# An attention decode kernel whose load order becomes K(n+1), V(n), with the values weighted one step later

## The chip, the cores and the metric

The kernel runs on one core of one Trainium2 chip. The metric is device time in microseconds (us) of one execution; lower is better. Before the change the median of three runs is 1319.77 us (1319.67 to 1320.77).

## What is computed

One decode step of a transformer block, batch 4, one query token, 32 heads of 128, a cache of 4096 positions, everything in float32:

```python
mod = (_silu(c) @ w_mod).reshape(c.shape[0], 6, 1, -1)
h = _layernorm(x, axis=-1) * (1 + ca) + sa
q = (h @ wq).reshape(B, Sq, H, Dh).transpose(0, 2, 1, 3)
scores = jnp.einsum("bhqd,bhkd->bhqk", q, k_cache) * (Dh ** -0.5)
p = _softmax(scores, axis=-1)
o = jnp.einsum("bhqk,bhkd->bhqd", p, v_cache)
x = x + ga * (o.transpose(0, 2, 1, 3).reshape(B, Sq, H * Dh) @ wo)
h = _layernorm(x, axis=-1) * (1 + cb) + sb
x = x + gb * (_silu(h @ w1) @ w2)
```

The two caches are 4 x 32 x 4096 x 128 floats, 268 MB each. Everything else is small beside them.

## The kernel before, in words

**Tiles.** The caches are cut into N = 32 steps. Step n takes one batch entry (b = n mod 4) and one group of four heads (t = n div 4); its K tile and its V tile are [128 partitions, 128 positions x 128] floats each, that is 128 x 16384 x 4 bytes = 8.39 MB. I call them K0 to K31 and V0 to V31 (k0, v0 and so on in the listings; the profile leaves the number out).

**Slots.** One such tile fills 64 KB of each partition, and the pool `kv` has three slots. Every big load is a `Slot`: the modulation weights `wm` (first, with the small work tiles of the opening behind them), `wq`, then the K and V tiles, then `wo`, then the FFN weights `w12`. A new slot takes the place of the one that came free first, so a load waits until the last reader of the load three places earlier in the order is done. All loads are issued by SyncE (SP), in the order of the program, in `fetch` (line 85); a load that waits holds up those behind it.

**A step.** In the K part, POOL multiplies the first 40 positions by the query and DVE the other 88 (`mult`, line 280), and DVE sums all of them over the head dimension (`red`, line 285, once for 88 and once for 40). The query that DVE reads is in PSUM (`qb`), that of POOL is a copy in SBUF (`qw`, line 275). Then comes the softmax: a row maximum on DVE (`rowmax`, line 289), a transpose on PE (`bmax`, line 293), three small DVE operations (`negmax`, lines 298 to 301) and the exponential on ACT (`softexp`, line 307); POOL then spreads the weights into the two tiles `pz` (line 311), from which PE takes its stationary operands. In the V part, POOL weights and folds the first 32 positions (`vmult`, lines 323 and 327), PE multiplies the other 96 by `pz` (`pv`, line 348) and adds the folded part with one more matmul (`vsum`, line 333). The last two steps leave all 128 positions to PE. `gather`, `norm` and `spread` turn the sums of a head group into the rows that the output projection reads (`project_a`, `project`).

**Order.** The order on each engine is that in which the program is written (`manual_schedule`). In step n the loop issues the load of K(n+1) first, does the K part and the softmax of n, issues the load of V(n+1), and does the V part of n. `vsum(n - 1)` stands behind the multiplications of step n. So the transfers are K0 V0 K1 V1 ... K31 V31, `wo`, `w12`. K31 is loaded and multiplied in two halves. `w12` comes in nine pieces of falling size, because the last matmuls of the FFN wait for the last of them.

Of the kernel before, what the change touches and what calls it, by code (L numbers as in the profile page):

```python
# [9 lines left out]
F32 = mybir.dt.float32  # L10
# [7 lines left out]
def kernel(  # L18
# [10 lines left out]
    nc = tc.nc  # L29
    P = 128  # L30
    B, H, S, Dh = kc.shape
# [7 lines left out]
    NT = H // HP  # L39
    TA = NT // 2  # L40
    QA = P // (HP * TA)
    RA = Dh // QA
    NJ = HP * S // P
# [6 lines left out]
    NI = F // P  # L50
    FG = F // G
    NA = 40
    NL = 56
    NV = 32
    SCALE = 1.0 / math.sqrt(Dh)
    EPS = 1e-5
    N = B * NT
# [4 lines left out]
    work = ctx.enter_context(tc.tile_pool(name="work", bufs=2))  # L62
# [24 lines left out]
    kt, vt = {}, {}  # L87

    def load(dst, cache, name, n, *cuts):
        t, b = divmod(n, B)  # L90
        dst[n] = Slot(f"{name}{n}").take(NJ, Dh)
        src = cache[b, HP * t : HP * (t + 1)].rearrange("h (p j) d -> (h p) j d", p=QW)
        fetch(dst[n], src, *(cuts or (0, NJ)))

    def load_k(n, *cuts):
        load(kt, kc, "k", n, *cuts)

    def load_v(n):
        load(vt, vc, "v", n)

    s0 = Slot("wm")
    cT, xT = s0.take(NK, B), s0.take(NK, B)
# [160 lines left out]
    qb, qw = {}, {}  # L263

    def make_qb(n):
        if n % B == 0:
            m = work.tile([P, B, Dh], F32, tag="o", name=f"qm{n}", bufs=1)
            for b in range(B):
                nc.scalar.activation(m[:, b, :], qn, AF.Copy, scale=sel[:, n + b : n + b + 1])  # L269
            p = psum([P, B, Dh], "q", 2)  # L270
            nc.tensor.matmul(p, blk.rearrange("p i x -> p (i x)"), m, start=True, stop=True)  # L271
            for b in range(B):
                qb[n + b] = p[:, b, :]
        qw[n] = work.tile([P, Dh], F32, tag="qw", name=f"qw{n}")
        nc.scalar.activation(qw[n], qb[n], AF.Copy)  # L275

    sc, nm, po, rs = {}, {}, {}, {}

    def mult(eng, src, n, lo, hi):
        eng.tensor_mul(  # L280
            kt[n][:, lo:hi, :], kt[n][:, lo:hi, :], src[n].unsqueeze(1).to_broadcast([P, hi - lo, Dh])
        )

    def red(n, lo, hi):
        nc.vector.tensor_reduce(sc[n][:, lo:hi], kt[n][:, lo:hi, :], axis=AX.X, op=ALU.add)  # L285

    def rowmax(n):
        nm[n] = work.tile([P, 1], F32, tag="rm", name=f"rm{n}")
        nc.vector.tensor_reduce(nm[n], sc[n], axis=AX.X, op=ALU.max)  # L289

    def bmax(n):
        p = psum([P, P], "mx", 2)
        nc.tensor.transpose(p, nm[n].to_broadcast([P, P]), ident)  # L293
        nm[n] = p

    def negmax(n):
        m = work.tile([P, HP], F32, tag="hx", name=f"hx{n}")
        nc.vector.tensor_reduce(m, nm[n].rearrange("p (i x) -> p i x", i=HP), axis=AX.X, op=ALU.max)  # L298
        nc.vector.tensor_mul(m, m, hn)
        nm[n] = work.tile([P, 1], F32, tag="nm", name=f"nm{n}")  # L300
        nc.vector.tensor_reduce(nm[n], m, axis=AX.X, op=ALU.add)  # L301

    def softexp(n):
        t, b = divmod(n, B)
        if b == 0:
            rs[t] = work.tile([P, B], F32, tag="rs", name=f"rs{t}")
        nc.scalar.activation(sc[n], sc[n], AF.Exp, bias=nm[n], accum_out=rs[t][:, b : b + 1])  # L307
        for h in range(2):
            f = first(n) if h == 0 else 0
            m = HG - f  # L310
            nc.gpsimd.tensor_mul(  # L311
                pz[h][:, f * W : HG * W].rearrange("p (g x) -> p g x", g=m)[:, :, E:].rearrange("p g (i j) -> p g i j", i=HP),
                sc[n][:, JJ * (HG * h + f) : HG * JJ * (h + 1)].rearrange("p (g j) -> p g j", j=JJ)
                .unsqueeze(2).to_broadcast([P, m, HP, JJ]),
                hm.unsqueeze(1).unsqueeze(3).to_broadcast([P, m, HP, JJ]),
            )

    def first(n):
        return NV // JJ if n < N - 2 else 0

    def vmult(n):
        if first(n):
            nc.gpsimd.tensor_mul(  # L323
                vt[n][:, :NV, :], vt[n][:, :NV, :], sc[n][:, :NV].unsqueeze(2).to_broadcast([P, NV, Dh])
            )
            for m in (NV // 2, NV // 4, JJ):
                nc.gpsimd.tensor_add(vt[n][:, :m, :], vt[n][:, :m, :], vt[n][:, m : 2 * m, :])  # L327

    def vsum(n):
        t, b = divmod(n, B)  # L330
        q, a = divmod(b, 2)
        o = (1 - a) * E
        nc.tensor.matmul(  # L333
            po[t, q][0:W, :], hs[:, o : o + W], vt[n][:, :JJ, :].rearrange("p j d -> p (j d)"),
            start=False, stop=a == 1,
        )

    def pv(n):
        t, b = divmod(n, B)
        q, a = divmod(b, 2)  # L340
        if a == 0:
            po[t, q] = psum([P, JJ * Dh], "po", 2)
        f = first(n)
        for j in range(f, NG):
            g = j % G
            h, u = divmod(j, HG)
            o = u * W + (1 - a) * E
            nc.tensor.matmul(  # L348
                po[t, q][W * g : W * (g + 1), :],
                pz[h][:, o : o + W],  # L350
                vt[n][:, JJ * j : JJ * (j + 1), :].rearrange("p j d -> p (j d)"),
                start=(a == 0 and j < f + G), stop=(a == 1 and j >= NG - G and (g > 0 or not f)),
            )
# [45 lines left out]
    def spread(t):  # L399
        if t < TA:  # L400
            g = slice(W * t, W * (t + 1))
            v = work.tile([P, B, QA, RA], F32, tag="o", name="v", bufs=1)
            nc.vector.tensor_mul(
                v[g], od[t][g].rearrange("p b (q r) -> p b q r", q=QA),
                rd[t][g].unsqueeze(3).to_broadcast([W, B, QA, RA]),
            )
            nc.vector.tensor_reduce(oa[g], v[g].rearrange("p b q r -> p r b q"), axis=AX.X, op=ALU.add)
            return
        on = work.tile([P, R, QW], F32, tag="lnu", name="on", bufs=1)
        nc.vector.tensor_scalar(  # L410
            on, od[t].rearrange("p (x r) -> p r x", r=R), rd[t][:, 1:2], None, op0=ALU.mult
        )
        ot = work.tile([P, R, W], F32, tag="o", name="ot", bufs=1)
        nc.vector.transpose(ot, on)
        nc.vector.tensor_copy(oz[:, t - TA], ot[:, :, :B])
# [9 lines left out]
    def project(lo, hi):  # L425
        for t in range(lo - TA, hi - TA):
            for r in range(R):
                nc.tensor.matmul(
                    accp[W * r : W * r + B, :], oz[:, t, r, :], wot[:, t, r, :],
                    start=False, stop=t == NT - TA - 1,  # L430
                )

    make_qb(0)
    load_v(0)
    for n in range(N):
        t, b = divmod(n, B)
        if n < N - 2:
            load_k(n + 1)
        elif n == N - 2:
            load_k(n + 1, 0, NJ // 2, NJ)  # L440
        else:
            so = Slot("wo")
            wat, wot = so.take(RA, D), so.take(NT - TA, R, D)
            fetch(so.t, wo, 0, RA * D, SLOT - R * D, SLOT)
        sc[n] = work.tile([P, NJ], F32, tag="sc", name=f"sc{n}")
        if n + 1 < N:
            mult(nc.gpsimd, qw, n, 0, NA)
            mult(nc.vector, qb, n, NA, NJ)
            make_qb(n + 1)
            if n and first(n - 1):  # L450
                vsum(n - 1)
            red(n, NA, NJ)
        else:
            for lo in (0, NJ // 2):
                mid, hi = lo + NL // 2, lo + NJ // 2
                mult(nc.gpsimd, qw, n, lo, mid)
                mult(nc.vector, qb, n, mid, hi)
                red(n, mid, hi)
        if n + 1 < N:
            red(n, 0, NA)  # L460
        else:
            for lo in (0, NJ // 2):
                red(n, lo, lo + NL // 2)
        rowmax(n)
        bmax(n)
        negmax(n)
        if t and b == 1:
            spread(t - 1)
        softexp(n)
        if n + 1 < N:  # L470
            load_v(n + 1)
        else:
            s2 = Slot("w12")
            w1t = s2.take(NK, F)
            w2t = s2.take(NI, D)
            fetch(s2.t, w12, 0, 3 * F, *(NK * F + i * D for i in (0, 5, 8, 10, 11, 12, 13, 14)))
        if b == B - 1:
            norm(t)
        vmult(n)
        pv(n)  # L480
        if n and b == 0:
            gather(t - 1, 1)
        if b == 2:
            gather(t, 0)
    project_a()
    gather(NT - 1, 1)
    project(TA, NT - 1)
    spread(NT - 1)
    project(NT - 1, NT)

    x1, hg, y = (s2.take(P) for _ in range(3))
    h2T, hid, th, hidT = s2.take(NK, W), s2.take(FG), s2.take(FG), s2.take(NI, W)
# [81 lines left out]
```

## Time and profile before

| | before |
|---|---|
| median of 3 runs | 1319.77 us |
| the profiled execution, its own time | 1319.19 us |
| its span, first to last instruction | 1317.4 us |
| DVE busy | 1017.4 us (77%) |
| POOL busy | 842.8 us (64%) |
| PE busy | 377.2 us (29%) |
| read from HBM | 567.30 MB |

The span is 1.8 us shorter than the time of the same execution. All rows that follow come from this one execution. In the timeline's rows the first number is the start in us from the beginning of the span, the second the duration, or, where a row stands for several (x2), the stretch that they take; in brackets stands how long the engine had been idle and what ended it. "SPq" is the queue of SyncE, and an L85 row there is a load being issued, not its transfer.

### The profile page before, as it was taken

What the parts mean: (1) busy time and instruction counts of PE and PEld (TensorE: products, weight loads), DVE (VectorE), ACT (ScalarE), POOL (GpSimd) and SP (SyncE); (2) the same over time, 40 slices, a digit from 0 to 9 for tenths busy, and PEclk for the clock granted to TensorE, in tenths of its full rate; (3) what the DMA queues carried; (4) which work ended last, traced back from release to release, by engine and by line L of the source; (5) the groups of instructions that cost most, each with busy time, mean ns of one, the idle gap of its engine ahead of it and who ended that gap; (6) DMA issues with size and microseconds to landing.
All of it is one profiled execution on the core that took longest, in us unless ns stands there. A gap on an engine that the chain in (4) does not pass through costs nothing.

```text
span 1317.4 us, 5420 instructions
## 1 busy us (share of the span) xinstructions
PE 377.2 (29%) x2114; PEld 94.6 (7%) x2114; DVE 1017.4 (77%) x361; ACT 51.5 (4%) x164; POOL 842.8 (64%) x227
## 2 busy tenths in 40 slices
PE   3421133223123232212332321332331233222138
PEld 1100000000000000000000000000000000000013
DVE  2378877777987777898777788777779877777982
ACT  1100000000000000000000000000000000000001
POOL 0236687666678666668866666876666787666650
PEclk9755566665566666556666555666655666655569
DMA  9999999999999999999999999999999999999998
GB/s 414 440 420 444 432 430 438 428 438 437 424 442 438 424 438 436 432 438 433 432 436 430 433 440 430 434 436 434 436 430 438 434 431 436 432 432 438 424 434 342
DMA packets 11433, 567.65 MB, mean 431 GB/s; under 512 B 1280, under 2 KB 1296, under 8 KB 2192
## 3 DMA queue, kind: packets, MB, share of 16 engines
q1 hardware_dynamic: 11408, 567.31, 99.5%
q8 instruction: 17, 0.28, 0.1%
q14 instruction: 8, 0.07, 0.0%
HBM read 567.30 MB, written 0.01 MB: 431 GB/s over the span
## 4 chain that ended last, share of the span: by engine, by line
DVE 36%; DMA 35%; POOL 19%; another core or an unknown queue 3%; PE 3%; issue 2%; ACT 1%; DVEq 0%; POOLq 0%; ACTq 0%
DMA k<-in_A_k_cache_dram 31%; DVE sc L285 21%; DVE k L280 14%; POOL v L327 9%; POOL v L323 8%; DMA w<-in_B_w_dram 3%; PE po L333 2%; DMA wm<-in_head_dram 1%; POOL pz L311 1%; POOL k L280 1%; ACT sc L307 1%; PE mx L293 1%; DVE hx L298 0%; DVE rm L289 0%
## 5 line engine op out<-in xcount | busy, mean ns | idle before, releaser
L285 DVE TENSOR_REDUCE sc<-k 128x88 f32<-128x11264 f32 (+2 forms) x66 | 553.1, 8422 | 1.1
L280 DVE TENSOR_TENSOR k<-k,q 128x11264 f32<-128x11264 f32 (+1 forms) x33 | 378.4, 11468 | 214.7 <-DMA k<-in_A_k_cache_dram 214.7
L280 POOL TENSOR_TENSOR k<-k,qw 128x5120 f32<-128x5120 f32 (+1 forms) x33 | 356.3, 10799 | 39.1 <-DMA k<-in_A_k_cache_dram 39.1
L311 POOL TENSOR_TENSOR pz<-sc,hm 128x128 f32<-128x128 f32 (+1 forms) x64 | 31.5, 512 | 376.9 <-ACT sc L307 376.9
L348 PE MATMUL po<-v,pz 128*32 128x512 f32 x1568 | 241.9, 781 | 44.9 <-POOL pz L311 44.8
L327 POOL TENSOR_TENSOR v<-v 128x2048 f32<-128x2048 f32 (+2 forms) x90 | 244.6, 2718 | 7.1
L323 POOL TENSOR_TENSOR v<-v,sc 128x4096 f32<-128x4096 f32 x30 | 210.9, 7031 | 0.0
L293 PE MATMUL mx<-ident,rm 128*128 128x128 f32 x32 | 14.5, 453 | 612.7 <-DVE rm L289 612.7
L333 PE MATMUL po<-v,hs 128*32 128x512 f32 x60 | 57.4, 1060 | 235.0 <-POOL v L327 235.0
L348 PEld LDWEIGHTS po<-v,pz 128*32 128x32 f32 x1568 | 56.6, 139 | 208.6 <-issue 156.2
L293 PEld LDWEIGHTS mx<-ident,rm 128*128 128x128 f32 x32 | 5.8, 181 | 664.9 <-issue 503.3
L307 ACT ACTIVATE sc<-sc,nm 128x128 f32<-128x128 f32 x32 | 12.8, 401 | 667.9 <-DVE nm L301 667.9
L275 ACT ACTIVATE qw<-q 128x128 f32<-128x128 f32 x32 | 8.9, 277 | 481.8 <-DVE k L280 454.2
L298 DVE TENSOR_REDUCE hx<-mx 128x4 f32<-128x128 f32 x32 | 9.3, 292 | 19.7 <-PE mx L293 19.7
L333 PEld LDWEIGHTS po<-v,hs 128*32 128x32 f32 x60 | 5.4, 140 | 257.9 <-POOL v L327 257.9
L359 DVE TENSOR_TENSOR o<-po,jm 128x512 f32<-128x512 f32 x16 | 10.9, 682 | 8.1 <-PE po L348 8.1
L365 DVE TENSOR_REDUCE s<-o 128x128 f32<-128x512 f32 x16 | 16.7, 1043 | 0.6
L199 PE MATMUL q<-wm 128*32 128x512 f32 x48 | 8.8, 665 | 18.8 <-DVE wm L183 18.8
L269 ACT ACTIVATE qm<-qn,sel 128x128 f32<-128x128 f32 x32 | 10.2, 390 | 31.2 <-PE od L370 27.7
L271 PE MATMUL q<-qm,blk 128*128 128x512 f32 x16 | 8.7, 625 | 7.2 <-ACT qm L269 7.2
L189 POOL COPY wm<-wm 128x16 f32<-128x16 f32 x1 | 0.2, 211 | 16.0 <-DMA wm<-in_head_dram 16.0
L183 DVE SCALAR_TENSOR_TENSOR wm<-wm 128x16 f32<-128x16 f32 x1 | 0.2, 189 | 12.8 <-ACT wm L182 12.8
(113 smaller groups left out, 153.2 us busy)
## 6 DMA issues: line engine op xcount, KB each, us to landing
k<-in_A_k_cache_dram SPq DMA_DIRECT2D x2, 4096.0 KB, 22.3
wm<-in_head_dram SPq DMA_DIRECT2D x1, 6160.0 KB, 17.6
wo<-in_A_wo_dram SPq DMA_DIRECT2D x1, 4096.0 KB, 26.8
wo<-in_A_wo_dram SPq DMA_DIRECT2D x1, 3072.0 KB, 33.7
w<-in_B_w_dram SPq DMA_DIRECT2D x1, 2688.0 KB, 23.8
w<-in_B_w_dram SPq DMA_DIRECT2D x1, 1280.0 KB, 28.1
wo<-in_A_wo_dram SPq DMA_DIRECT2D x1, 1024.0 KB, 35.7
w<-in_B_w_dram SPq DMA_DIRECT2D x4, 256.0 KB, 17.5
```

The source lines that it names most:

```text
L269: nc.scalar.activation(m[:, b, :], qn, AF.Copy, scale=sel[:, n + b : n + b + 1])
L280: eng.tensor_mul(kt[n][:, lo:hi, :], kt[n][:, lo:hi, :], src[n].unsqueeze(1).to_broadcast([P, hi - lo, Dh]))
L285: nc.vector.tensor_reduce(sc[n][:, lo:hi], kt[n][:, lo:hi, :], axis=AX.X, op=ALU.add)
L293: nc.tensor.transpose(p, nm[n].to_broadcast([P, P]), ident)
L307: nc.scalar.activation(sc[n], sc[n], AF.Exp, bias=nm[n], accum_out=rs[t][:, b : b + 1])
L311: nc.gpsimd.tensor_mul(pz[h][:, f * W : HG * W].rearrange("p (g x) -> p g x", g=m)[:, :, E:].rearrange("p g (i j) -> p g i j", i=HP), sc[n ...
L323: nc.gpsimd.tensor_mul(vt[n][:, :NV, :], vt[n][:, :NV, :], sc[n][:, :NV].unsqueeze(2).to_broadcast([P, NV, Dh]))
L327: nc.gpsimd.tensor_add(vt[n][:, :m, :], vt[n][:, :m, :], vt[n][:, m : 2 * m, :])
L333: nc.tensor.matmul(po[t, q][0:W, :], hs[:, o : o + W], vt[n][:, :JJ, :].rearrange("p j d -> p (j d)"), start=False, stop=a == 1,)
L348: nc.tensor.matmul(po[t, q][W * g : W * (g + 1), :], pz[h][:, o : o + W], vt[n][:, JJ * j : JJ * (j + 1), :].rearrange("p j d -> p (j d)") ...
L359: nc.vector.tensor_mul(o, po[t, q].rearrange("p (j d) -> p j d", j=JJ), jm.unsqueeze(2).to_broadcast([P, JJ, Dh]))
L365: nc.vector.tensor_reduce(s, o.rearrange("p j d -> p d j"), axis=AX.X, op=ALU.add)
```

## The change

The load of V moves behind that of the next K, and the V part of step n - 1 is done in step n, after the multiplications of K(n). The order of transfers becomes K0 K1 V0 K2 V1 ... K31 V30 V31, `wo`, `w12`. K31 is now loaded and multiplied whole, and V31 in two halves. `wo` and `w12` are issued together after the sums of step 31. `vsum`, `gather`, `norm` and `spread` move to later places, and the output projection comes after everything else of the attention.

```diff
-    def load_k(n, *cuts):
-        load(kt, kc, "k", n, *cuts)
-    def load_v(n):
-        load(vt, vc, "v", n)
+    def load_k(n):
+        load(kt, kc, "k", n)
+    def load_v(n, *cuts):
+        load(vt, vc, "v", n, *cuts)
...
     make_qb(0)
-    load_v(0)
     for n in range(N):
         t, b = divmod(n, B)
-        if n < N - 2:
+        if n + 1 < N:
             load_k(n + 1)
-        elif n == N - 2:
-            load_k(n + 1, 0, NJ // 2, NJ)
+        else:
+            load_v(n, 0, NJ // 2, NJ)
+        sc[n] = work.tile([P, NJ], F32, tag="sc", name=f"sc{n}")
+        mult(nc.gpsimd, qw, n, 0, NA)
+        mult(nc.vector, qb, n, NA, NJ)
+        if n + 1 < N:
+            make_qb(n + 1)
+        if n:
+            vmult(n - 1)
+            pv(n - 1)
+        red(n, NA, NJ)
+        red(n, 0, NA)
+        if n + 1 < N:
+            load_v(n)
         else:
             so = Slot("wo")
...
-        sc[n] = work.tile([P, NJ], F32, tag="sc", name=f"sc{n}")
-        if n + 1 < N:
-            mult(nc.gpsimd, qw, n, 0, NA)
-            mult(nc.vector, qb, n, NA, NJ)
-            make_qb(n + 1)
-            if n and first(n - 1):
-                vsum(n - 1)
-            red(n, NA, NJ)
-        else:
-            for lo in (0, NJ // 2):
...
-        rowmax(n)
-        bmax(n)
-        negmax(n)
-        if t and b == 1:
-            spread(t - 1)
-        softexp(n)
-        if n + 1 < N:
-            load_v(n + 1)
-        else:
             s2 = Slot("w12")
...
-        if b == B - 1:
+        rowmax(n)
+        bmax(n)
+        if n and first(n - 1):
+            vsum(n - 1)
+        negmax(n)
+        softexp(n)
+        if b == 3:
+            gather(t, 0)
             norm(t)
-        vmult(n)
-        pv(n)
-        if n and b == 0:
+        if t and b == 1:
             gather(t - 1, 1)
-        if b == 2:
-            gather(t, 0)
+        if t and b == 2:
+            spread(t - 1)
+    pv(N - 1)
+    gather(NT - 1, 1)
+    spread(NT - 1)
     project_a()
-    gather(NT - 1, 1)
-    project(TA, NT - 1)
-    spread(NT - 1)
-    project(NT - 1, NT)
+    project(TA, NT)
```

On SP the head of the order of loads was this (a name's first number is the step; the second only tells buffers apart):

```order
L117 DMA wm_69<-in_head_dram 128x12320
L119 DMA wq_74<-in_A_wq_dram 128x16384
L85 DMA k0_76<-in_A_k_cache_dram 128x16384
L85 DMA v0_265<-in_A_v_cache_dram 128x16384 [waits DMAHW1_49,PE_49]
L85 DMA k1_267<-in_A_k_cache_dram 128x16384 [waits DVE_49,PE_49,DMAHW0_49,Activation_49,Pool_49]
L85 DMA v1_289<-in_A_v_cache_dram 128x16384 [waits DMAHW2_49,DVE_49]
L85 DMA k2_320<-in_A_k_cache_dram 128x16384 [waits DMAHW3_49,PE_49]
```

and is now this:

```order
L116 DMA wm_69<-in_head_dram 128x12320
L118 DMA wq_74<-in_A_wq_dram 128x16384
L84 DMA k0_76<-in_A_k_cache_dram 128x16384
L84 DMA k1_265<-in_A_k_cache_dram 128x16384 [waits DMAHW1_49,PE_49]
L84 DMA v0_274<-in_A_v_cache_dram 128x16384 [waits DVE_49,PE_49,DMAHW0_49,Activation_49,Pool_49]
L84 DMA k2_289<-in_A_k_cache_dram 128x16384 [waits DMAHW2_49,DVE_49]
L84 DMA v1_327<-in_A_v_cache_dram 128x16384 [waits DMAHW3_49,DVE_49]
L84 DMA k3_342<-in_A_k_cache_dram 128x16384 [waits DMAHW4_49,PE_49]
```

K1 and V0 have changed places. The fourth K/V load waited for DVE's last read of K0 (the transfer DMAHW2) in both; the fifth waited for PE's last read of V0, and is now V1, which waits for DVE's last read of K1 (DMAHW3).

On POOL steps 0 and 1 read so before, from the multiplication of K0 on:

```order
L280 TENSOR_TENSOR k0_76<-k0_76,qw0_263 128x5120
L311 TENSOR_TENSOR pz0_112<-sc0_269,hm_95 128x8x16
L311 TENSOR_TENSOR pz1_113<-sc0_269,hm_95 128x16x16
L323 TENSOR_TENSOR v0_265<-v0_265,sc0_269 128x4096
L327 TENSOR_TENSOR v0_265<-v0_265 128x2048
L327 TENSOR_TENSOR v0_265<-v0_265 128x1024
L327 TENSOR_TENSOR v0_265<-v0_265 128x512
L280 TENSOR_TENSOR k1_267<-k1_267,qw1_272 128x5120
L311 TENSOR_TENSOR pz0_112<-sc1_322,hm_95 128x8x16
```

and so now:

```order
L279 TENSOR_TENSOR k0_76<-k0_76,qw0_263 128x5120
L310 TENSOR_TENSOR pz0_112<-sc0_267,hm_95 128x8x16
L310 TENSOR_TENSOR pz1_113<-sc0_267,hm_95 128x16x16
L279 TENSOR_TENSOR k1_265<-k1_265,qw1_270 128x5120
L322 TENSOR_TENSOR v0_274<-v0_274,sc0_267 128x4096
L326 TENSOR_TENSOR v0_274<-v0_274 128x2048
L326 TENSOR_TENSOR v0_274<-v0_274 128x1024
L326 TENSOR_TENSOR v0_274<-v0_274 128x512
L310 TENSOR_TENSOR pz0_112<-sc1_291,hm_95 128x8x16
```

The four operations on V0 have moved behind the multiplication of K1, and so ahead of the weights of step 1.

On PE the matmuls of step 0's values and the transposition of step 1 (`mx<-ident,rm1`) stood so before:

```order
L293 MATMUL mx_278<-ident_78,rm0_276 128x128
L348 MATMUL po_295<-v0_265,pz0_112 32x512 x8
L348 MATMUL po_295<-v0_265,pz1_113 32x512 x16
L333 MATMUL po_295<-v0_265,hs_116 32x512
```

and stand so now:

```order
L292 MATMUL mx_278<-ident_78,rm0_276 128x128
L347 MATMUL po_300<-v0_274,pz0_112 32x512 x8
L347 MATMUL po_300<-v0_274,pz1_113 32x512 x16
L292 MATMUL mx_331<-ident_78,rm1_329 128x128
L332 MATMUL po_300<-v0_274,hs_116 32x512
```

The matmul that reads V0 last, and so sets its slot free, has moved behind the transposition of step 1's softmax.

More of the change, by code (lines that the diff above doesn't have):

```diff
@@ L52 @@
     NA = 40
-    NL = 56
     NV = 32
@@ L444 @@
             fetch(so.t, wo, 0, RA * D, SLOT - R * D, SLOT)
-        sc[n] = work.tile([P, NJ], F32, tag="sc", name=f"sc{n}")
-        if n + 1 < N:
-            mult(nc.gpsimd, qw, n, 0, NA)
-            mult(nc.vector, qb, n, NA, NJ)
-            make_qb(n + 1)
-            if n and first(n - 1):
-                vsum(n - 1)
-            red(n, NA, NJ)
-        else:
-            for lo in (0, NJ // 2):
[L455 to L458, printed above, removed]
-        if n + 1 < N:
-            red(n, 0, NA)
-        else:
-            for lo in (0, NJ // 2):
-                red(n, lo, lo + NL // 2)
-        rowmax(n)
-        bmax(n)
-        negmax(n)
-        if t and b == 1:
-            spread(t - 1)
-        softexp(n)
-        if n + 1 < N:
-            load_v(n + 1)
-        else:
             s2 = Slot("w12")
```

## The prediction

> **What bounds the kernel now.** I read the page's busy shares and DMA rows first, then a table of windows, then the timeline of the head and of the tail.
>
> ```profile
> DVE  2378877777987777898777788777779877777982
> DMA  9999999999999999999999999999999999999998
> q1 hardware_dynamic: 11408, 567.31, 99.5%
> 57.60:96.25 38.65, 7.17 (x45) 1.89 (x49) 30.07 (x8) 2.06 (x4) 18.20 (x4) 0.53 1.00 434
> 289.76:1219.10 929.34, 251.41 (x1280) 57.64 (x1276) 752.09 (x222) 30.38 (x108) 649.49 (x169) 0.59 1.00 434
> 1296.40:1313.70 17.30, 14.04 (x189) 7.81 (x182) 4.61 (x13) 3.96 (x6) 0.00 (x0) 0.90 0.87 360
> ```
>
> The last three rows are windows: stretch, length, busy time of PE, PEld, DVE, ACT and POOL, granted clock, DMA share, GB/s. The DMA share is 1.00 from the first K tile to the last steps, always at 434 GB/s, while DVE, the busiest engine, works 752 of 929 us. So the transfers are the bound, and an engine counts only where it keeps a load from being issued in time. The bytes do not change; the question is whether the queue ever runs dry.
>
> The head shows how the queue is fed:
>
> ```profile
> 0.74 0.38 SPq L117 DMA_DIRECT2D wm<-in_head_dram  x1
> 18.33 0.21 ACT L182 ACTIVATE wm<-wm 128x16 f32<-128x16 f32 x1 [16.31 <-DMA wm<-in_head_dram]
> 46.55 0.33 SPq L85 DMA_DIRECT2D v<-in_A_v_cache_dram  x1
> 48.63 0.33 SPq L85 DMA_DIRECT2D k<-in_A_k_cache_dram  x1
> 57.63 11.89 DVE L280 TENSOR_TENSOR k<-k,q 128x11264 f32<-128x11264 f32 x1 [22.43 <-DMA k<-in_A_k_cache_dram]
> 69.55 17.28 DVE L285 TENSOR_REDUCE sc<-k 128x88 f32<-128x11264 f32 x2
> 86.86 0.33 SPq L85 DMA_DIRECT2D v<-in_A_v_cache_dram  x1
> 88.31 0.16 DVE L301 TENSOR_REDUCE nm<-hx 128x1 f32<-128x4 f32 x1
> 89.07 0.97 POOL L311 TENSOR_TENSOR pz<-sc,hm 128x128 f32<-128x128 f32 x2 [20.36 <-ACT sc L307]
> 96.25 11.89 DVE L280 TENSOR_TENSOR k<-k,q 128x11264 f32<-128x11264 f32 x1 [7.79 <-DMA k<-in_A_k_cache_dram]
> 107.41 0.33 SPq L85 DMA_DIRECT2D k<-in_A_k_cache_dram  x1
> 1219.10 11.89 DVE L280 TENSOR_TENSOR k<-k,q 128x11264 f32<-128x11264 f32 x1 [7.06 <-DMA k<-in_A_k_cache_dram]
> ```
>
> Each DVE multiplication starts when its K tile lands. K0 lands at 57.63 and K30 at 1219.10, with 60 tiles after K0 in between: (1219.10 - 57.63) / 60 = 19.36 us a tile, 38.72 us a step. V0 goes out at 46.55, when `wq` has been read; K1 at 48.63; V1 at 86.86, at the end of the sums of K0 (69.55 + 17.28 = 86.83); K2 at 107.41, when PE is done with V0. With three slots, a tile has to be consumed within two tile times (38.7 us) of its landing, or the queue is empty. Now K takes 86.86 - 57.63 = 29.23 us, which leaves 9.5 us; V0 lands one tile after K0, at 77.0, and is set free at 107.41, 30.4 us later, which leaves 8.3.
>
> **The change, part by part.** These rows price it: groups by shape (count, busy us and mean ns of one, idle time before), two pieces of the timeline, and DMA issues (KB, median us from issue to landing):
>
> ```profile
> L280 DVE TENSOR_TENSOR k<-k,q 128x11264 f32<-128x11264 f32 x31 | 368.5, 11888 | 214.7 <-DMA k<-in_A_k_cache_dram 214.7
> L285 DVE TENSOR_REDUCE sc<-k 128x88 f32<-128x11264 f32 x31 | 368.5, 11886 | 1.1
> L280 POOL TENSOR_TENSOR k<-k,qw 128x5120 f32<-128x5120 f32 x31 | 340.7, 10992 | 39.1 <-DMA k<-in_A_k_cache_dram 39.1
> L323 POOL TENSOR_TENSOR v<-v,sc 128x4096 f32<-128x4096 f32 x30 | 210.9, 7031 | 0.0
> 97.11 8.30 POOL L327 TENSOR_TENSOR v<-v 128x2048 f32<-128x2048 f32 x3
> 105.46 1.91 PE L333 MATMUL po<-v,hs 128*32 128x512 f32 x2 [8.56 <-POOL v L327]
> L365 DVE TENSOR_REDUCE s<-o 128x128 f32<-128x512 f32 x16 | 16.7, 1043 | 0.6
> L359 DVE TENSOR_TENSOR o<-po,jm 128x512 f32<-128x512 f32 x16 | 10.9, 682 | 8.1 <-PE po L348 8.1
> wm<-in_head_dram SPq DMA_DIRECT2D x1, 6160.0 KB, 17.6
> v<-in_A_v_cache_dram SPq DMA_DIRECT2D x32, 28.6
> out_dram<-w SPq DMA_DIRECT2D x1, 8.0 KB, 1.8
> ```
>
> *The head.* K1 takes V0's place and lands at 57.63 + 19.36 = 76.99 instead of 96.25; V0 lands at 96.35; K2, issued at 86.86 when K0 has been read, at 115.71. Next in the queue is V1, which takes K1's slot and waits for DVE. DVE cannot start on K1 at 76.99: it reads K0 until 86.86 and ends the softmax at 88.31 + 0.16 = 88.47. The multiplication runs from 88.49 to 100.38, the sums to 100.40 + 17.28 = 117.68. (POOL multiplies its 40 positions from 89.07 + 0.97 = 90.04 to 101.03; the sums need them only at 112.3.) So V1 is issued at 117.70, 2.0 us after the only transfer in the queue has landed. Two K tiles have come back to back, 19.4 us apart, to an engine that takes 29.2 + 1.6 us for each.
>
> A load that meets an empty queue costs more than its tile time. `wm`, 6160 KB = 6.31 MB, went out at 0.74 into an empty queue and took 17.6 us; at 8.39 MB in 19.36 us = 433 GB/s its bytes need 14.56, so 3.0 us are start and end. V1 then lands at 117.70 + 3.0 + 19.36 = 140.06; in an unbroken stream it would have landed at 115.71 + 19.36 = 135.07. The difference, 5.0 us, is lost for good. The bounds of the 3.0: below, the output's 8 KB, which took 1.8 us altogether (then 3.8 us); above, `wm`, `wq` and K0 together, 23.09 MB or 53.3 us in 57.63 - 0.74 = 56.89, so 3.6 (then 5.6 us). I take 3.0: it is the same kind of load, first in an empty queue.
>
> The Trainium skill ("DMA: Bandwidth & Descriptors", section "Anatomy of one DMA") fits a fixed 2.0 us plus bytes at 436 GB/s for a DMA, on GpSimd's path. By that V1 would land at 117.70 + 2.0 + 19.24 = 138.94 and the loss would be 3.9 us, an estimate; this trace's first load has 1 us more.
>
> *The steps after it.* DVE catches up. The softmax of step 1 ends at 117.68 + 1.63 = 119.3, K2's sums at 148.5, and K3 lands at 140.06 + 19.36 = 159.4: V2 goes out 10.9 us ahead of that. From then on DVE starts on each K as it lands, and V(n) is issued 29.2 us later, with 38.7 - 29.2 = 9.5 us in hand, as now. K(n+2) waits for V(n-1). On POOL that tile lands 19.4 us into step n, behind 11.0 us of K work, and is folded by 19.4 + 7.03 + 8.30 = 34.7; `vsum`, now behind the transposition at about 30, ends at 36.6. K(n+2) is needed at 58.1, which leaves 21 us where it was 8.3. So the spare of one of the two kinds of load grows, of the other it stays; the queue was never dry, so this brings nothing. In step 1 the same chain is later: POOL is done with V0 at 101.03 + 15.3 = 116.4, `vsum` at 120.5, K3 goes out behind V1 and is in time.
>
> *What else moves.* The weights `pz` of step n now stand behind the fold of V(n-1) on POOL and are written at 35.7 instead of 31.5; PE needs them when V(n) lands at 58. `gather`, `norm` and `spread` (1.7 us of DVE for a `gather`) stay in the 7 us in which DVE waits for the next K. Cover gone, a late DVE still has the 9.5 us. All of this I cost at zero.
>
> *The tail.* These rows are of the last steps before:
>
> ```profile
> 1278.91 24.18 SPq L85 DMA_DIRECT2D w<-in_B_w_dram  x9
> 1290.25 3.61 PE L423 MATMUL acc<-wo,oa 128*4 128x512 f32 x32
> 1294.21 3.62 PE L428 MATMUL acc<-wo,oz 128*4 128x512 f32 x32
> 1312.34 0.16 PEld L525 LDWEIGHTS po<-w 128*32 128x32 f32 x8 [0.17 <-DMA w<-in_B_w_dram]
> 1313.05 0.16 PEld L525 LDWEIGHTS po<-w 128*32 128x32 f32 x8 [0.55 <-DMA w<-in_B_w_dram]
> 1313.68 0.16 PEld L525 LDWEIGHTS po<-w 128*32 128x32 f32 x8 [0.47 <-DMA w<-in_B_w_dram]
> ```
>
> The end hangs on the last pieces of `w12`, and the last four tiles come in another order but with the same bytes. K31 lands a tile earlier, so `wo` is issued 2 x 19.36 - 29.2 = 9.5 us and `w12`, right behind it, 29 us before its turn, and after V31's last half PE has half of one step's matmuls and DVE a `gather` and a `spread` before `wo` is there. The output projection ends with the landing of `wo`, as now. PE has been idle before it and may be granted half the clock (0.53 on average in the step at 57.60): the last 8 of 32 matmuls would take 0.9 us more (3.62 / 32 a matmul), against waits of 0.17 + 0.55 + 0.47 = 1.2 us for the last pieces. I take 0, bounds 0 and +0.9.
>
> *The sum.* 1317.4 + 5.0 = 1322.4 us of span. The profiled execution took 1319.19, 0.6 under the median of 1319.77; on the median I put 1319.8 + 5.0 = 1324.8 us, 0.38% slower. Of what can be told from no change (0.2%, 2.6 us) that is about twice.
>
> **The rivals.**
>
> *The loss is made up (same, or faster).* K tiles will be issued some 21 us before their turn instead of 8. If handing over from one transfer to the next costs something with a short queue, every second transfer gains. To cancel 5.0 us over 31 loads each has to gain 0.16 us, to be 0.2% faster 0.25 us (then 1317 us). Against it: the steady tile time of 19.36 us hides no hand-over; `wq` and K0, issued at the very start, took 57.63 - 18.33 = 39.3 us for the two, 19.65 each. The other way to "same" is a restart that costs under 0.7 us, below anything the rows show; 1320 to 1322 us.
>
> *A stall in every step (much slower).* The fold of V now runs while DVE sums and does its softmax, and V(n) goes out only after the sums. Should DVE become more than 9.5 - 3.0 = 6.5 us longer between the landing and the end of the sums, the queue is empty in each of 31 steps; one us beyond that is +31 us (1356). What speaks for two engines in each other's way is one pair of rows:
>
> ```profile
> 205.05 0.97 POOL L311 TENSOR_TENSOR pz<-sc,hm 128x128 f32<-128x128 f32 x2 [11.05 <-ACT sc L307]
> 205.53 0.53 DVE L387 TENSOR_TENSOR ra<-dx,dqm 32x32 f32<-32x32 f32 x1
> ```
>
> A DVE operation of 32 x 32 takes 0.53 us and ends at 206.06, just when POOL's ends (206.02). The Trainium skill ("SBUF — State Buffer", section "Who interferes with whom") says that a DVE instruction with two SBUF inputs and a GpSimd instruction that reads SBUF exclude each other for a whole instruction, and one with a single SBUF input is free; the two rows agree. Against the stall: the big DVE operations take 11.89 and 17.28 us in the first step, beside POOL's K work, and 11.89 at 96.25, beside POOL's fold at 97.11; all 31 average 11.888. Only the small operation at line 299 may now wait behind a fold, up to 7.0 us; it comes after the sums, and DVE has 7 us until the next K. I give it little.
>
> **How the numbers follow.** One idle stretch at the head, 1323.3 to 1326.9 (3.8 to 5.6 us, up to 0.9 of tail, half a us of spread): 0.79. Made up to within 0.2%: 0.10. Faster: 0.04. A stall that comes back, in part or in every step: 0.07. So slower 0.86, same 0.10, faster 0.04. The range takes the first case, the upper end of the second (1322.2) and small recurring losses to 1327.5.
>
> **What would show it.** The second V load issued at about 117.7, and about 22.4 us from issue to its landing, where V loads have a median of 28.6 (they queue behind another). A dip of the DMA rate in the fourth slice. K2 landing near 115.7, K3 near 159.4, then a K every 38.7. The first DVE wait for K goes: multiplications of K0, K1 and K2 follow each other with only the softmax between. DVE's two big operations keep 11.89 and 17.28 us. The tail after the last piece of `w12` unchanged, everything 5 us later. I am wrong if V1 goes out before 115, if the steps are not 38.7 us long afterwards, or if PE's last matmuls no longer wait for `w12`.

## The result, and the profile after

The changed kernel takes 1324.99 us (median of six runs, 1324.79 to 1326.01) against 1319.82 us in the same runs of the kernel before: 5.17 us or 0.4% slower, ratio 1.004 with a 95% interval of 1.0027 to 1.0053. The forecast was 1324.8. The profiled execution of the changed kernel took 1325.08 us, its span 1323.3, which is 5.9 more than the span before; of two single executions that is within the spread of the runs.

The page of the changed kernel has the loss in one place. These are its rows on DVE and DMA, and GB/s in the 40 slices:

```profile
DVE  2399789787878988788897878788887889978861
DMA  9998999999999999999999999999999999999998
GB/s 413 438 426 372 415 440 440 418 442 438 420 440 440 436 428 434 440 426 434 436 430 436 436 436 434 430 436 434 430 435 434 436 434 434 434 432 434 434 424 348
q1 hardware_dynamic: 11408, 567.31, 99.2%
```

The fourth slice (99 to 132 us) has 372 GB/s; it had 444 before. The slices after it swing about the same mean as before, and the window from 290.00 below has 434 GB/s again. The windows of the prediction, taken again (columns as there, the last two the DMA share and GB/s):

```profile
57.60:96.25 38.65, 0.45 (x1) 0.18 (x1) 37.80 (x8) 2.06 (x4) 18.16 (x4) 0.50 1.00 434
96.25:135.19 38.94, 10.10 (x51) 2.42 (x51) 38.13 (x9) 1.05 (x4) 31.93 (x8) 0.59 0.89 377
290.00:1224.00 934.00, 251.40 (x1272) 64.33 (x1272) 767.66 (x222) 30.37 (x108) 650.54 (x168) 0.59 1.00 434
```

DVE is busy for 37.8 of the first 38.65 us, where it had 30.1, and the DMA share of the next window is 0.89. Afterwards it is 1.00 at 434 GB/s as before. The timeline shows the hand-over itself:

```profile
86.91 0.33 SPq L84 DMA_DIRECT2D k<-in_A_k_cache_dram  x1
88.47 11.89 DVE L279 TENSOR_TENSOR k<-k,q 128x11264 f32<-128x11264 f32 x1
100.39 17.28 DVE L284 TENSOR_REDUCE sc<-k 128x88 f32<-128x11264 f32 x2
117.70 0.33 SPq L84 DMA_DIRECT2D v<-in_A_v_cache_dram  x1
120.40 0.33 SPq L84 DMA_DIRECT2D k<-in_A_k_cache_dram  x1
139.52 7.04 POOL L322 TENSOR_TENSOR v<-v,sc 128x4096 f32<-128x4096 f32 x1 [7.72 <-DMA v<-in_A_v_cache_dram]
160.15 11.89 DVE L279 TENSOR_TENSOR k<-k,q 128x11264 f32<-128x11264 f32 x1 [8.80 <-DMA k<-in_A_k_cache_dram]
1320.71 0.59 SPq L518 DMA_DIRECT2D out_dram<-w  x1
```

DVE goes from K0 straight on to K1, without the wait for the DMA that it had at 96.25 before. V1 is issued when the sums of K1 end, at 117.70, and has landed at 139.5; DVE starts on K3 at 160.15. K2, issued at 86.91, has 28.6 us from issue to landing in the trace, so it landed at 115.5. The rates in steps of 2 us:

```profile
110.00:112.00 2.00, 0.00 (x0) 0.00 (x0) 2.00 (x1) 0.00 (x0) 2.00 (x1) 0.50 0.98 426
112.00:114.00 2.00, 0.00 (x0) 0.00 (x0) 2.00 (x2) 0.00 (x0) 1.92 (x2) 0.50 0.31 131
114.00:116.00 2.00, 0.00 (x0) 0.00 (x0) 2.00 (x1) 0.00 (x0) 1.92 (x2) 0.50 0.00 0
116.00:118.00 2.00, 0.00 (x0) 0.00 (x0) 1.96 (x2) 0.00 (x0) 0.46 (x1) 0.50 0.00 0
118.00:120.00 2.00, 1.96 (x3) 0.36 (x3) 1.38 (x4) 0.49 (x2) 0.16 (x1) 0.50 1.53 524
```

A window counts a packet whole, in the stretch in which it begins; that is how the last row comes to a share of 1.53. A packet, the piece in which the queue moves data, is 65.5 KB here (8.39 MB in 128), and 131 GB/s over 2 us are four of them, of about 2.5 us each by the share of 0.31. So K2's last four packets begin between 112 and 114, and the data flow until about 115, just before the landing. Then the queue is empty: nothing begins until 118, when V1's first packets do. After that the shift stays: the output is issued at 1320.71, 5.9 us later than the 1314.82 of before, and it was 5.7 at K3 (160.15 - 57.69 = 102.46 us behind K0, for five tiles of 19.36 = 96.8). The tail waits for the same things as before:

```profile
1299.87 3.62 PE L427 MATMUL acc<-wo,oz 128*4 128x512 f32 x32 [2.02 <-DMA wo<-in_A_wo_dram]
1319.57 0.16 PEld L512 LDWEIGHTS po<-w 128*32 128x32 f32 x8 [0.47 <-DMA w<-in_B_w_dram]
```

### The profile page after: what moved, and what is told of

It is laid out like the page before. It is cut to its first block, busy times and chain, and to the rows that moved or that the text cites. A ratio compares the mean times of both kernels' runs of the same rounds, so it can differ in the third digit from the quotient of the medians.

```text
span 1323.3 us, 5424 instructions
## 1 busy us (share of the span) xinstructions
PE 379.6 (29%) x2114; PEld 102.9 (8%) x2114; DVE 1032.7 (78%) x358; ACT 51.4 (4%) x164; POOL 839.5 (63%) x226
## 4 chain that ended last, share of the span: by engine, by line
DMA 57%; DVE 27%; POOL 11%; PE 2%; another core or an unknown queue 2%; issue 0%; SPq 0%; DVEq 0%; ACT 0%; POOLq 0%
DMA k<-in_A_k_cache_dram 31%; DMA v<-in_A_v_cache_dram 21%; DVE sc L284 16%; DVE k L279 11%; POOL v L326 6%; POOL v L322 5%; DMA w<-in_B_w_dram 3%; PE po L332 1%; DMA wm<-in_head_dram 1%; PE q L198 1%; DVE wm L206 0%; PE q L210 0%; SPq L84 0%; PE od L369 0%
## 5 line engine op out<-in xcount | busy, mean ns | idle before, releaser
L284 DVE TENSOR_REDUCE sc<-k 128x88 f32<-128x11264 f32 x64 | 552.9, 8681 | 3.2
L279 DVE TENSOR_TENSOR k<-k,q 128x11264 f32<-128x11264 f32 x32 | 380.4, 11887 | 172.8 <-DMA k<-in_A_k_cache_dram 172.8
L279 POOL TENSOR_TENSOR k<-k,qw 128x5120 f32<-128x5120 f32 x32 | 353.0, 11032 | 130.0 <-DMA k<-in_A_k_cache_dram 130.0
L347 PEld LDWEIGHTS po<-v,pz 128*32 128x32 f32 x1568 | 64.5, 139 | 816.0 <-issue 816.0
L292 PE MATMUL mx<-ident,rm 128*128 128x128 f32 x32 | 11.1, 346 | 135.9 <-DVE rm L288 135.9
L298 DVE TENSOR_TENSOR hx<-hx,hn 128x4 f32<-128x4 f32 x32 | 15.8, 495 | 1.1
L270 PE MATMUL q<-qm,blk 128*128 128x512 f32 x16 | 15.4, 1061 | 1.7 <-ACT qm L268 1.7
## 6 DMA issues: line engine op xcount, KB each, us to landing
w<-in_B_w_dram SPq DMA_DIRECT2D x1, 1280.0 KB, 37.8
```

The lines of the kernel that those rows point to most:

```text
L279: eng.tensor_mul(kt[n][:, lo:hi, :], kt[n][:, lo:hi, :], src[n].unsqueeze(1).to_broadcast([P, hi - lo, Dh]))
L347: nc.tensor.matmul(po[t, q][W * g : W * (g + 1), :], pz[h][:, o : o + W], vt[n][:, JJ * j : JJ * (j + 1), :].rearrange("p j d -> p (j d)") ...
```

## Experiments

Two theories stood against each other: A, the loss is the idle stretch at the head and moves one for one with the moment at which V1 can be issued; B, it comes from the new order elsewhere, in the steps or in the tail. The runs of one group are compared with the kernel before in the same runs on the same chip (1319.4 to 1319.6 us).

### The head, longer and shorter

The first three runs change only how K0 and K1 are shared between POOL and DVE:

```diff
-        mult(nc.gpsimd, qw, n, 0, NA)
-        mult(nc.vector, qb, n, NA, NJ)
+        na = {0: 24, 1: 24}.get(n, NA)
+        mult(nc.gpsimd, qw, n, 0, na)
+        mult(nc.vector, qb, n, na, NJ)
...
-        red(n, NA, NJ)
-        red(n, 0, NA)
+        red(n, na, NJ)
+        red(n, 0, na)
```

> The changed kernel, but in steps 0 and 1 POOL multiplies 24 positions of K instead of 40 and DVE 104 instead of 88. Theory A (the whole loss is the one idle stretch at the head, set by when DVE has summed K1): DVE needs 16 x 128 elements = 2.16 us more in each of the two steps, V1 goes out at 122.0 instead of 117.7, and everything behind it is 4.3 us later: 1329.3 us. Rival B (the loss is made in the steps after or in the tail, the head only moves things about): 1325 us as before this edit.

Measured: 1328.92 us, 9.3 over the kernel before (ratio 1.0071, 1.0058 to 1.0084).

> The changed kernel with 52 positions of K on POOL in steps 0 and 1 instead of 40. Theory A: DVE is 1.6 us shorter in each of the two, V1 goes out at 114.4, 1.3 us before K2 lands at 115.7, and lands at 114.4 + 21.8 = 136.2 instead of 139.5: 3.3 us of the loss come back, 1321.7 us. Rival B: 1325 us.

Measured: 1321.75 us, 2.1 over (1.0015, 1.0006 to 1.0024).

> The changed kernel with 64 positions of K on POOL in step 0 and 56 in step 1 instead of 40. Theory A: V1 goes out at about 112.7, 3.0 us before K2 lands, which is the whole price of a restart; the queue does not run dry and nothing is lost: 1320.0 us, the time of the kernel before. Rival B: 1325 us.

Measured: 1321.03 us, 1.4 over (1.001, 1.0001 to 1.0019). The issue of V1 in the three, from their timelines:

```profile
122.06 0.33 SPq L84 DMA_DIRECT2D v<-in_A_v_cache_dram  x1
```

```profile
114.49 0.33 SPq L84 DMA_DIRECT2D v<-in_A_v_cache_dram  x1
```

```profile
113.44 0.33 SPq L84 DMA_DIRECT2D v<-in_A_v_cache_dram  x1
116.40 11.89 DVE L279 TENSOR_TENSOR k<-k,q 128x11264 f32<-128x11264 f32 x1 [1.28 <-DMA k<-in_A_k_cache_dram]
136.68 7.04 POOL L322 TENSOR_TENSOR v<-v,sc 128x4096 f32<-128x4096 f32 x1 [6.11 <-DMA v<-in_A_v_cache_dram]
157.63 11.89 DVE L279 TENSOR_TENSOR k<-k,q 128x11264 f32<-128x11264 f32 x1 [9.12 <-DMA k<-in_A_k_cache_dram]
```

V1 4.4 us later costs 4.1 us more (9.3 against 5.2), 3.2 us earlier gives 3.1 back. Nothing in the steps or in the tail was touched, so B falls for all but a rest. The third run shows the rest: V1 goes out 2.9 us before K2 lands (at 116.3, DVE starts on it at 116.40), and 1.4 us are still lost, where theory A had expected none. V1 lands 20.3 us behind K2 and K3 another 21.0 behind that, together 2.5 over two tile times; the profiled execution took 1322.21 us, 2.6 over the kernel before, so its loss lies at the head too. Either a restart needs a longer lead than 3.0 us, or this rest belongs to B.

To lengthen the lead, POOL was to multiply 80 positions of K1, and that ahead of the weights of step 0 (in the other steps they stay at the end of `softexp`):

```diff
...
-        mult(nc.gpsimd, qw, n, 0, NA)
-        mult(nc.vector, qb, n, NA, NJ)
+        na = {0: 64, 1: 80}.get(n, NA)
+        mult(nc.gpsimd, qw, n, 0, na)
+        mult(nc.vector, qb, n, na, NJ)
+        if n == 1:
+            weights(0)
...
```

> The changed kernel with 64 positions of K on POOL in step 0 and 80 in step 1; POOL multiplies K1 ahead of the weights of step 0 (V0 lands only at 96.4, so they are not yet needed). DVE then has summed K1 at about 110.1 and V1 goes out 5.6 us before K2 lands, against 3.0 us in the run with 64 and 56, where 1.4 us of the loss were left. Theory A (a restart needs a longer lead than I put, because the 16 DMA engines are idle before the landing shows): the rest of the loss goes, 1319.6 to 1320.3 us. Rival B (1.4 us of the loss are not the idle stretch, but the order or the tail): 1321.0 us again.

Measured: 1330.45 us (1.0081, 1.0067 to 1.0095), worse than any other of this group. Its timeline has the reason:

```profile
77.72 21.74 POOL L279 TENSOR_TENSOR k<-k,qw 128x10240 f32<-128x10240 f32 x1 [1.82 <-DMA k<-in_A_k_cache_dram]
85.90 13.58 DVE L298 TENSOR_TENSOR hx<-hx,hn 128x4 f32<-128x4 f32 x1
99.62 6.55 DVE L279 TENSOR_TENSOR k<-k,q 128x6144 f32<-128x6144 f32 x1
123.52 0.33 SPq L84 DMA_DIRECT2D v<-in_A_v_cache_dram  x1
```

A DVE multiplication of four elements a partition, 0.16 us in the kernel before and 1.60 at most in the changed one, lasts 13.58 us and ends at 99.48, with POOL's (99.46). It reads `hx` and `hn`, both in SBUF. The large multiplication of DVE, which has the query in PSUM, keeps its pace beside POOL's: it takes 11.89 us in every step. The rule of the Trainium skill that the prediction weighed ("SBUF — State Buffer", "Who interferes with whom": two SBUF inputs on DVE and a GpSimd instruction that reads SBUF exclude each other for a whole instruction) is what one would read here; the test is to put one operand in PSUM and leave the rest:

```diff
-        p = psum([P, P], "mx", 2)
-        nc.tensor.transpose(p, nm[n].to_broadcast([P, P]), ident)
+        p = psum([P, P + HP], "mx", 2)
+        nc.tensor.transpose(p[:, :P], nm[n].to_broadcast([P, P]), ident)
...
+        h = nm[n][:, P:]
+        nc.vector.tensor_reduce(h, nm[n][:, :P].rearrange("p (i x) -> p i x", i=HP), axis=AX.X, op=ALU.max)
         m = work.tile([P, HP], F32, tag="hx", name=f"hx{n}")
-        nc.vector.tensor_reduce(m, nm[n].rearrange("p (i x) -> p i x", i=HP), axis=AX.X, op=ALU.max)
-        nc.vector.tensor_mul(m, m, hn)
+        nc.vector.tensor_mul(m, h, hn)
```

> The run with 64 and 80 positions on POOL again, with one thing changed: the four maxima of the softmax are written to PSUM instead of SBUF, so that the small DVE multiplication by the mask reads one operand from SBUF and not two. Theory L (that multiplication waited 13.4 us for POOL's multiplication of K1 because both read SBUF): it is back at 0.16 us, V1 goes out at about 110.1, 5.6 us before K2 lands, and with theory A the rest of the loss goes: 1319.6 to 1320.3 us. Rival B (1.4 us of the loss are the order or the tail): 1321.0 us. Rival M (DVE waited for something else of POOL): 1330 us again.

Measured: 1319.44 us against 1319.46 (0.9999, 0.999 to 1.0008). The same place now:

```profile
78.18 21.79 POOL L279 TENSOR_TENSOR k<-k,qw 128x10240 f32<-128x10240 f32 x1 [1.82 <-DMA k<-in_A_k_cache_dram]
86.37 0.16 DVE L299 TENSOR_TENSOR hx<-mx,hn 128x4 f32<-128x4 f32 x1
110.86 0.33 SPq L84 DMA_DIRECT2D v<-in_A_v_cache_dram  x1
116.73 11.89 DVE L279 TENSOR_TENSOR k<-k,q 128x11264 f32<-128x11264 f32 x1 [4.48 <-DMA k<-in_A_k_cache_dram]
136.00 7.04 POOL L327 TENSOR_TENSOR v<-v,sc 128x4096 f32<-128x4096 f32 x1 [7.86 <-DMA v<-in_A_v_cache_dram]
155.36 11.89 DVE L279 TENSOR_TENSOR k<-k,q 128x11264 f32<-128x11264 f32 x1 [7.87 <-DMA k<-in_A_k_cache_dram]
L299 DVE TENSOR_TENSOR hx<-mx,hn 128x4 f32<-128x4 f32 x32 | 5.2, 162 | 1.1
```

The multiplication runs in the midst of POOL's, and the wait is gone (theory L). V1 goes out 5.8 us before K2 lands, the tiles follow at 19.3 and 19.4 us, and nothing of the loss is left, within an interval of 0.1% or 1.3 us. The maxima in PSUM do not bring this by themselves: the last run of this document has them too, with the head of the change, and stays at 1325.69 (one run). So all of the loss was the head, and the new order in the other steps and in the tail costs nothing that these runs can tell. Set in order of V1's lead over K2's landing (K2's issue plus the time from issue to landing that each trace has for it):

| kernel | V1 issued | lead, us | over the kernel before, us |
|---|---|---|---|
| 64, 80 positions on POOL, maxima in SBUF | 123.52 | -7.4 | 11.0 |
| 24, 24 | 122.06 | -6.5 | 9.3 |
| the change (40, 40) | 117.70 | -2.2 | 5.2 |
| 52, 52 | 114.49 | 1.0 | 2.1 |
| 64, 56 | 113.44 | 2.9 | 1.4 |
| 64, 80, maxima in PSUM | 110.86 | 5.8 | 0.0 |

### One half of the change without the other

The later values with the old order of loads:

```diff
     make_qb(0)
+    load_v(0)
     for n in range(N):
...
-        else:
-            load_v(n, 0, NJ // 2, NJ)
...
-            load_v(n)
+            load_v(n + 1)
```

> The later values alone: the load order is that of before (V(n) ahead of K(n+1)), and the values of step n - 1 are done in step n as in the changed kernel. Here the slots go V to V and K(n) to K(n+1): K(n+1) waits for DVE's last read of K(n), 29.3 us after its landing, while the queue has ended with V(n) 19.4 us after it. Theory A: the queue runs dry in each step, K(n+1) lands 29.3 + 21.8 = 51 us after K(n) instead of 38.7: about 1700 us. Rival C (the place of the values decides nothing as long as the transfers come in their old order): 1320 us.

Measured: 1721.68 us (one run). DVE's waits for K in the middle of it:

```profile
615.09 11.89 DVE L279 TENSOR_TENSOR k<-k,q 128x11264 f32<-128x11264 f32 x1 [19.57 <-DMA k<-in_A_k_cache_dram]
666.33 11.89 DVE L279 TENSOR_TENSOR k<-k,q 128x11264 f32<-128x11264 f32 x1 [16.29 <-DMA k<-in_A_k_cache_dram]
```

A step of 51.2 us, as expected; about every second one is a us longer.

The new order of loads with the values in their own step:

```diff
-        if n:
-            vmult(n - 1)
-            pv(n - 1)
...
-        if n and first(n - 1):
-            vsum(n - 1)
         negmax(n)
         softexp(n)
+        if n + 1 < N:
+            vmult(n)
+            pv(n)
+            if first(n):
+                vsum(n)
```

> The new load order alone: K(n+1) is loaded ahead of V(n), but POOL and PE do the values of step n in step n, right behind its weights, as before the change (V31 at the end, as in the changed kernel). Now the slots go K to K and V to V: V(n) waits for the last reader of V(n-1). Theory A: at the head V1 goes out at 96.3 + 15.3 + 1.9 = 113.7, 2 us before K2 lands, so little is lost there; but in each step V(n) goes out 17.4 us after V(n-1) has landed and K(n+1) lands 2.0 us after that, so of the 2.4 to 3.0 us of a restart 0.4 to 1.0 stay open 30 times: 1332 to 1350 us. Rival C (a load that is issued at all before the one in front has landed costs nothing): 1320 us.

Measured: 1488.21 us (1.1272, 1.1245 to 1.1299). That is far more than expected, and the trace puts most of it in every fourth step, where `norm` now stood behind a wait for V:

```profile
597.09 10.96 POOL L279 TENSOR_TENSOR k<-k,qw 128x5120 f32<-128x5120 f32 x1
599.22 0.18 DVE L385 RECIPROCAL dx<-mx 32x4 f32<-32x4 f32 x1 [24.11 <-PE po L332]
599.44 8.66 DVE L386 TENSOR_TENSOR ra<-dx,dqm 32x32 f32<-32x32 f32 x1
```

DVE waits 24.1 us for PE, and then 8.66 us in an operation of 32 x 32 with two operands in SBUF, up to the end of POOL's. So the edit itself had put something in the way, and I made it again with the values behind `gather`, `norm` and `spread`:

> The new load order alone once more, with gather, norm and spread now ahead of the values on PE and DVE, so that they do not wait for a V (in the first try this wait of DVE took some 20 us in every fourth step). Values of step n in step n. Theory A: what is left is V(n) waiting for the last reader of V(n-1), which leaves it some 2 us ahead of the end of the queue: the ordinary steps of the first try were 39.3 to 41.5 us long instead of 38.7, so 1340 to 1390 us. Rival C (the whole 168 us of the first try come with the order): 1480 us.

Measured: 1387.24 us (one run), 67.8 over, about 2.2 us for each step; from one multiplication of V to the next it is 39.3 to 42.2 us. One of the longer ones:

```profile
667.38 7.04 POOL L322 TENSOR_TENSOR v<-v,sc 128x4096 f32<-128x4096 f32 x1 [6.53 <-DMA v<-in_A_v_cache_dram]
684.78 0.33 SPq L84 DMA_DIRECT2D v<-in_A_v_cache_dram  x1
709.05 7.04 POOL L322 TENSOR_TENSOR v<-v,sc 128x4096 f32<-128x4096 f32 x1 [6.62 <-DMA v<-in_A_v_cache_dram]
```

V is issued 17.4 us after the one before has landed, some 2 us ahead of the landing of the K in between (issued at 657.61, 29.1 us to landing), and the next V lands 41.7 us after the last instead of 38.7. Neither half is of use alone: with three slots the order of the loads and the order in which they are set free have to fit each other.

### What the later values are good for

The prediction says that V's slot now has 21 us in hand instead of 8.3. Two more additions in each fold were to use 9.1 us of that (they took 7.3), first in the kernel before, then in the changed one:

```diff
             for m in (NV // 2, NV // 4, JJ):
                 nc.gpsimd.tensor_add(vt[n][:, :m, :], vt[n][:, :m, :], vt[n][:, m : 2 * m, :])
+                if m == NV // 2:
+                    for _ in range(2):
+                        nc.gpsimd.tensor_add(vt[n][:, m : 2 * m, :], vt[n][:, m : 2 * m, :], vt[n][:, m : 2 * m, :])
```

> The kernel before, with two more additions of 2048 elements a partition by POOL in each fold of V (on positions that are no longer read), 9.1 us more ahead of the last reader of V. Theory A: before the change the load of K has 8.3 us in hand behind V's last reader, so it now comes too late in each step, and POOL's K work moves back as well: a step of about 43 us, 1400 to 1480 us. Rival D (the spare of 8.3 us is more, or the queue is not filled by this chain): 1320 us.

Measured: 1427.48 us (one run), 108 over; the steps are 42.2 us long:

```profile
409.26 10.97 POOL L280 TENSOR_TENSOR k<-k,qw 128x5120 f32<-128x5120 f32 x1
428.91 7.03 POOL L323 TENSOR_TENSOR v<-v,sc 128x4096 f32<-128x4096 f32 x1
434.53 11.89 DVE L280 TENSOR_TENSOR k<-k,q 128x11264 f32<-128x11264 f32 x1 [5.48 <-DMA k<-in_A_k_cache_dram]
451.51 10.97 POOL L280 TENSOR_TENSOR k<-k,qw 128x5120 f32<-128x5120 f32 x1
```

The time is within theory A's range, but a late K is not what sets it. The second K has landed by 434.53, and POOL comes to it 17 us later without a wait. POOL goes round in a loop: K's products for 11.0 us, DVE's sum of them and the softmax until 428.91, V's products and the fold until 451.5, and then the next K. Without the additions it would take 42.2 - 7.3 = 34.9 us, within the step of 38.7, and with them it does not fit. The 8.3 us in hand behind V's last reader would have shrunk to 1.0, worth some 2 us a step by the table above and not the 3.5 measured. In the changed kernel the fold belongs to the step before and does not wait for the softmax of this one. The small multiplications keep 0.16 us here, so they have no part in the 108.

> The changed kernel with the same two more additions by POOL in each fold of V. Theory A: here the load of K has 21 us in hand behind V's last reader, of which 9.1 go; POOL's step is 27.1 + 9.1 = 36.2 us of 38.7, and V's load hangs on DVE's sums, which do not change: 1325 us, as without them. Rival D: slower by the same as the kernel before with these additions, since POOL is the engine that gets longer: 1400 us or more.

Measured: 1366.89 us (one run): 61 us better than the kernel before with the same load, but 42 us over the change without it, so neither theory has it. A fourth step again:

```profile
695.46 10.96 POOL L279 TENSOR_TENSOR k<-k,qw 128x5120 f32<-128x5120 f32 x1
696.67 0.19 DVE L388 RECIPROCAL dx<-mx 32x4 f32<-32x4 f32 x1 [11.21 <-PE po L335]
696.89 9.58 DVE L389 TENSOR_TENSOR ra<-dx,dqm 32x32 f32<-32x32 f32 x1
```

DVE waits for the matmuls of `norm`, which stand on PE behind `vsum` and so behind the fold, and then for POOL's multiplication. The last run takes both away: maxima as above and the reciprocals of `norm` in PSUM, and

```diff
+        negmax(n)
+        softexp(n)
+        if b == 3:
+            gather(t, 0)
+            norm(t)
         if n and first(n - 1):
             vsum(n - 1)
-        negmax(n)
-        softexp(n)
-        if b == 3:
-            gather(t, 0)
-            norm(t)
```

> The changed kernel with the two more additions in each fold, with the maxima and the reciprocals in PSUM (no DVE multiplication with two operands in SBUF there) and with gather and norm ahead of the matmul that reads V last, so that DVE does not wait for POOL in every fourth step. If the 47 us that the longer fold cost were these waits, 1325 to 1330 us; if they were POOL's own time, 1365 us again.

Measured: 1325.69 us (one run), as the change without the additions. The operation is short again, now in the midst of a fold on POOL:

```profile
192.60 7.28 POOL L330 TENSOR_TENSOR v<-v 128x2048 f32<-128x2048 f32 x2
196.43 0.18 DVE L390 TENSOR_TENSOR ra<-mx,dqm 32x32 f32<-32x32 f32 x1
L390 DVE TENSOR_TENSOR ra<-mx,dqm 32x32 f32<-32x32 f32 x4 | 0.7, 187 | 0.1
```

So, with these waits gone, the changed order carries the longer fold at no cost, and the kernel before pays 108 us for it. By the trace of the latter it is POOL's loop that makes the difference; whether the 21 us of V's slot were needed as well, these runs do not tell. Either way the spare has no use in this kernel as it stands, where nothing was late.

## Why the prediction was right

**The bound.** The DMA queue was full before and is full after, save at one place. The step stays at 38.7 us, DVE's two large operations at 11.89 and 17.28 us.

**The moment of V1.** Forecast 117.70, measured 117.70: K0, the softmax, K1 in a row, each from its own row of the trace. K2 was put at 115.71 and landed at 115.5. That K2 would be the last transfer in the queue followed from the slots, and the run with 24 positions (V1 at 122.06) moved the loss with it.

**The size.** 5.0 us forecast, 5.17 measured, but not made as I had put it. V1 took 21.8 us from its issue, so start and end are 2.4 us and not 3.0; by V1's landing only 4.4 us were lost (139.52, against 57.69 + 4 x 19.36 = 135.1). K3 then came 20.6 us behind V1, 1.3 more than a tile, and that I had not foreseen. The two errors nearly cancel, so that the number came out this close is in part luck. My 3.0 us from `wm` are too much for start and end: they were 2.4 to 2.6 in the three runs in which V1 met an empty queue (21.8, 21.9 and 22.0 us from issue to landing). The Trainium skill's 2.0 us ("DMA: Bandwidth & Descriptors", section "Anatomy of one DMA") lie about as far below them as the 3.0 above, and the estimate of 3.9 us for the loss that rested on it falls short, above all by the part that comes after.

**How early is early enough.** The sum implies that a load issued 3.0 us before the queue ends costs nothing. That step was wrong: at 2.9 us 1.4 were left, at some 2 us (order alone) some 2.2 in each step, at 5.8 nothing. The traces show why the landing is a poor mark for the end. They count a landing in 16 steps, as many as there are DMA engines, and it is complete with the last; in the run with 64 and 56 positions K2's steps come from 113.96 to 116.30, in the last of the table from 113.98 to 116.64. So part of the queue has nothing to do 2.3 to 2.7 us before the landing. And V1's first packets begin 1.0 us after its issue. Together that asks for a lead of 3.3 to 3.7 us, an estimate from these figures; no run has a lead between 2.9 and 5.8.

**The steps and the tail.** Costed at zero, and zero within the spread of the runs: from K3 to K30 a step is 38.72 us in both traces ((1219.10 - 173.60) / 27 and (1205.62 - 160.15) / 27), and the run without the head's loss equals the kernel before. The output projection waits for `wo`, the last matmuls for `w12`, as forecast.

**The rivals.** The loss was not made up, nor did the stall in every step come. The group of K loads among the DMA issues of the changed kernel (the last column is the median from issue to landing), and, by its line, the durations of the small multiplication (min, median and max in ns):

```profile
k<-in_A_k_cache_dram SPq DMA_DIRECT2D x32, 40.6
```

```profile
L298 DVE TENSOR_TENSOR hx<-hx,hn x32: 161/490/1601, 88.2 to 1274.8; 128x4 f32<-128x4 f32 x32
```

K loads are issued a median of 40.6 us before they land, where it was 27.5, and the tile time did not change. The small multiplication, which may wait for POOL, takes 1.60 us at most. I had put its limit at 7.0 us, the longest operation of the fold, and given it little weight because of its place behind the sums; one step of POOL's K work moved forward made it 13.6 us, on the path.

## What to carry to other kernels

In a stream through three buffers, count for every load which reader sets its slot free and how long before the end of the queue that is; the first steps need their own count, because there two tiles of the dear kind can come back to back (here K) and leave a hole that is never filled again. A load in hand for 8 us is as good as one for 21 when nothing is late, so an order that adds spare gives no time, and it shows its worth only when POOL's work grows. Before moving work of GpSimd under that of VectorE, look for small VectorE operations with two operands in SBUF: here one of 0.16 us became 13.6, and an operand in PSUM cured it.

## What the runs showed of the hardware

- A VectorE multiplication with both operands in SBUF lasted until the end of a GpSimd multiplication that ran beside it: 13.58, 8.66 and 9.58 us instead of 0.16 to 0.19. With one operand in PSUM the first and the last were short again (0.16 and 0.18 us), in the midst of GpSimd's work. In the kernel before, the 32 x 32 one took 0.52 us in all four cases, beside POOL's 0.97; it is 0.18 in the changed kernel, where POOL rests beside it.
- A load of 8.39 MB into an empty queue took 21.8 to 22.0 us in three runs, 2.4 to 2.6 more than in the stream. In the changed kernel its first packets begin 1.0 us after the issue and take 2.6 to 3.4 us instead of 2.4.
- The tile after it was late too, by 1.1 to 1.6 us in the five runs in which V1 came late. The 16 steps of the landings show where this comes from: in the changed kernel K2's spread over 1.61 us, V1's, whose packets begin almost together, over 0.46, and K3's over 1.66 again; with 64 and 56 positions it is 2.34, 1.89 and 3.43. The spread that comes back is the delay of the last step. Why it comes back is open.
- To hide a restart wholly the load had to be issued more than 2.9 and at most 5.8 us before the one in front had landed.
